# Attention and two gated layers in float32 parts: the products with w1, w2 and w_in by Strassen's scheme

## The chip, the cores and the metric

One core of a Trainium2 chip runs the whole program. The metric is device microseconds from start to end of one launch. The engines are named as in the profile: PE (TensorE matmuls) with PEld (its weight loads), DVE (VectorE), ACT (ScalarE), POOL (GpSimd) and SP (SyncE, which issues the transfers).

## The reference

```
scores = q @ k^T / 8, causal mask, softmax over keys, @ v   # 2 batches x 12 heads, 448 tokens, width 64
x = heads side by side                  # 896 tokens x 768
x = ((x @ w1) * (x @ w2)) @ w3 @ w_out  # w1, w2 768x1024, w3 1024x1024, w_out 1024x768
g = relu(x @ w_in) ** 2                 # w_in 768x2048
out = g @ w_out2                        # 2048x768
```

The weights arrive as 64-bit floats and are rebuilt as 32-bit ones on the chip. Each large product is done in a float32 variant of PE (F32R) on operands split into a high and a low part, as three matmuls: high by high, high by low, low by high.

## The kernel before

**Attention and W.** Thirteen slots (the loop `for p in range(SLOTS)`) each handle one pair of heads: `scores(p)`, `minima` (DVE: mask and row extreme), `exps` (ACT), `divide` (POOL, or DVE for the last pair's second head), and for the pair before, `p_transposes` (PE, copied out by ACT) and `attend`, whose result `x_parts` (L285) splits into the two parts of `xT`, in slots of 448 tokens per batch. Between them PE computes W = w3 @ w_out in 32 half units (`w_half`, L293, of which `fill` hands out one or none at each of three places of a slot); DVE adds them into `wraw` in SBUF. The 16 pieces of w3 and 8 of w_out, and then the first of w1 and w2, are loaded and converted step by step (`step`, `convert`, L83): ACT and DVE rebuild float32 from the 64-bit words (L102, L103, L108), ACT casts the high part (L90), DVE subtracts for the low part (L106). In this stage PE, DVE and ACT each run in the order of the code (`manual_schedule`); POOL and SP, and everything later, are ordered by a planner.

**w1 and w2** (`w12`, `ab`). For each of 8 column blocks m, PE multiplies the 6 row blocks of w1, then those of w2, by both batches of `xT`, 3 matmuls of 448 columns each: 576 matmuls. ACT copies the w1 result out of PSUM (L489), DVE multiplies (L490), ACT casts (L119) and POOL subtracts (L120) into `abT`. The first two m take batch 0 first (`EARLY`), so that the last pair of heads is not yet needed.

**h** (`h_parts`). 288 matmuls of 448 columns, W against `abT`.

**Last layer.** Two groups of d_ff: 8 blocks of w_in (288 matmuls of 448 columns; ACT takes ReLU, square and high part, POOL the low part), then 336 matmuls of 384 columns with w_out2, added into `acc`.

Weights wait in a ring of 8 tiles of both parts; `used` converts the next one when one is free. Two groups begin with a `pause` (one float32 matmul of 64 columns).

Of the kernel before, what the change touches and what calls it, by code (L numbers as in the profile page):

```python
# [8 lines left out]
F32 = mybir.dt.float32  # L9
F32R = mybir.dt.float32r  # L10
# [7 lines left out]
def attention_moe_moe2(ctx: ExitStack, tc: tile.TileContext, qk, v, w1, w2, w3, w_out, w_in2, w_out2, out):  # L18

# [21 lines left out]
    KD = DM // P  # L41
    KF = w1.shape[0]
# [6 lines left out]
    RING = 8  # L49
# [11 lines left out]
    ringp = ctx.enter_context(tc.tile_pool(name="ring", bufs=RING))  # L61
    ps_w = ctx.enter_context(tc.tile_pool(name="ps_w", bufs=2, space=PSUM))
    rawp = ctx.enter_context(tc.tile_pool(name="raw", bufs=RAW))

    xT = big.tile([P, 2, KD, NT], F32R, tag="X", name="xT")
    wraw = big.tile([P, KF, DM], F32, tag="W", name="wraw")

    def mm(o, l, r, start, stop):
        return nc.tensor.matmul(o, l, r, start=start, stop=stop)  # L69


    raws, f32s = {}, {}
# [8 lines left out]
    def convert(a=None, b=None):  # L81

        if b:  # L83
            nm, n = b
            if nm == "w3":
                t = w3_tile(n)
            else:
                t = ringp.tile([P, 2, DM], F32R, tag="ring", name=f"hl_{nm}_{n}")
            x = wraw[:, n, :] if nm == "W" else f32s[b] if whole(b) else f32s.pop(b)
            nc.scalar.copy(t[:, 0], x)  # L90
            hls[b] = t
        if a:
            raw = raws.pop(a)
            n = raw.shape[1]
            low, high = raw[:, :, 0], raw[:, :, 1]
            if whole(a) and a[0] == "w3":
                y = w3_tile(a[1])[:, 0].bitcast(F32)
            elif whole(a):
                y = w3p[0].tile([P, DM], F32, tag="xw", name=f"xw_{a[1]}", bufs=NB)
            else:  # L100
                y = rawp.tile([P, DM], F32, tag="x", name=f"x_{a[0]}_{a[1]}", bufs=XB)[:, :n]
            nc.scalar.activation(y, high.bitcast(F32), AF.Prelu, scale=2.0 ** -112, alpha=-2.0 ** 32)  # L102
            nc.vector.tensor_scalar(low, low, 2.0 ** -29, 7.0, ALU.mult, ALU.min)  # L103
            f32s[a] = y
        if b:
            nc.vector.tensor_tensor(t[:, 1], x, t[:, 0].bitcast(F32), op=ALU.subtract)  # L106
# [4 lines left out]
    def whole(key):  # L111

        return key[0] == "w3" and key[1] < PLAIN or key[0] == "wout" and key[1] < NB

    def w3_tile(n):
        return w3p[0].tile([P, 2, W3N], F32R, tag="w3", name=f"w3_{n}", bufs=2)
# [23 lines left out]
    order += ring[KF:]  # L140
    source = {"wout": w_out, "w1": w1, "w2": w2, "w3": w3, "win2": w_in2, "wout2": w_out2}
    place = {key: i for i, key in enumerate(order)}
    in_ring = {key: i for i, key in enumerate(ring)}
    hls = {}
    made = {"load": 0, "f32": 0, "hl": 0}

    def make_loads(n):
        for key in order[made["load"]:n]:
            if key[0] != "W":
                load(key, source[key[0]][key[1]])  # L150
        made["load"] = max(made["load"], min(n, len(order)))

    def make_f32(n):
        for key in order[made["f32"]:n]:
            make_loads(made["f32"] + 1)
            if key[0] != "W":
                convert(key)
            made["f32"] += 1

    def make(key):  # L160

        while made["hl"] <= place[key]:
            i = made["hl"]
            at = order[i]
            make_f32(i + 2)
            make_loads(i + 2 + RAW)
            convert(b=at)
            made["hl"] += 1

    def used(key):  # L170

        n = in_ring[key] + RING
        if n < len(ring):
            make(ring[n])

    w3p = []


    with (
        tc.tile_pool(name="attq", bufs=2) as attq,  # L180
        tc.tile_pool(name="att", bufs=2) as att,
        tc.tile_pool(name="attc", bufs=1) as attc,
        tc.tile_pool(name="ps_a", bufs=6, space=PSUM) as ps_a,
    ):
        ident = attc.tile([P, P], F32, tag="ident", name="ident")
# [112 lines left out]
        w3p.append(attc)  # L298
        x_t = {}

        def w_half(g, i, n):
# [3 lines left out]
            for f in range(NB):  # L305
                c = slice(f * P, (f + 1) * P)
                if n3 < PLAIN:
                    mm(acc, f32s["w3", n3][:, c], f32s["wout", f][:, cols], f == 0, f == NB - 1)
                    continue
                t, wo = hls["w3", n3], hls["wout", g * NB + f]  # L310
                for s, r in ((0, 0), (0, 1), (1, 0)):
                    mm(acc, t[:, s, c], wo[:, r, cols],
                       f == 0 and (s, r) == (0, 0), f == NB - 1 and (s, r) == (1, 0))
# [6 lines left out]
        units = [(g, i, n) for g in range(N3 // KF) for i in range(KF) for n in range(2)]  # L320
        NU = len(units)


        parts = [key for key in order if not (key[0] == "w3" and key[1] < PLAIN)]
        steps = [0, 0]

        def free(key):
# [3 lines left out]
            k = in_ring.get(key, 0) - RING  # L331
            return k < 0 or k < NB and done[1] >= NU // 2

        def ahead(n):

            last = max(order.index(key) for key in LENT)
            return max(n + RAW, min(n + RAW + len(LENT), last + 1 + RAW))

        def step(f32=True, split=True):
            a, b = order[steps[0]], parts[steps[1]]  # L340
            spare = sum(not whole(k) for k in f32s) < XB
            b = b if split and b in f32s and free(b) else None
# [270 lines left out]
```

## Time and profile before

| | |
|---|---|
| three runs | 577.06, 577.17, 577.54 us; median 577.17 |
| profiled execution | span 575.4 us from first to last instruction; its own time is not listed apart, the median run stands 1.8 us above this span |
| granted PE clock | 1.000 on the mean |
| attention and W | 0 to 163.2 us |
| w1, w2 | 163.2 to 280.2 us |
| h | 280.2 to 338.5 us |
| last layer | 338.5 to 572.1 us, then the last add and the last store |

The page gives busy time by engine, the span in 40 slices, the chain of work that ended last, and the costliest groups. A group has line, engine, operation, result and inputs, shapes and count; behind the bar stand total busy time, mean ns of one, and the idle time before. Neighbouring instructions of an engine overlap at their ends, so the step from one start to the next is a little shorter than a duration.

### The profile page before, as it was taken

To read this page: it belongs to the slowest core of one execution; us is meant where nothing else is said; L and a number is where in the kernel's file an instruction comes from. 1 tells how busy PE (TensorE), PEld (TensorE's weight loads), DVE (VectorE), ACT (ScalarE), POOL (GpSimd) and SP (SyncE) were. 2 spreads that over 40 slices of the span, in tenths; PEclk is the share of its full clock that TensorE was granted. 3 is DMA by queue.
4 is the path that set the end of the run, shared out by engine and by line. 5 is a ranking of instruction groups with operands and counts; after the bars stand their busy time and mean duration, and the time that the engine had idled before them with its cause. 6 is when DMAs were issued, how large, how long until landed. Compare 5 with 4: busy or idle time off the path is not lost.

```text
span 575.4 us, 8129 instructions
## 1 busy us (share of the span) xinstructions
PE 563.9 (98%) x3144; PEld 506.5 (88%) x3144; DVE 281.3 (49%) x567; ACT 268.2 (47%) x574; POOL 159.1 (28%) x140
## 2 busy tenths in 40 slices
PE   7899999999999999999999999999999999999997
PEld 5557777778989999999999999999999999999997
DVE  5987887767687544222210484555102854421011
ACT  5778777757865533222210456666002666640000
POOL 3367677776200312111100003333000023330000
PEclk9999999999999999999999999999999999999999
DMA  8854554233266633000000274333100763000111
GB/s 318 288 194 140 177 159 159 84 124 120 88 225 245 204 120 107 9 1 1 1 1 0 67 271 156 109 111 110 56 1 4 270 219 110 1 1 29 56 55 56
DMA packets 14823, 63.96 MB, mean 111 GB/s; under 512 B 1665, under 2 KB 1921, under 8 KB 14785
## 3 DMA queue, kind: packets, MB, share of 16 engines
q1 hardware_dynamic: 14784, 63.45, 32.2%
q8 instruction: 25, 0.41, 0.3%
q14 instruction: 14, 0.11, 0.1%
HBM read 60.69 MB, written 2.75 MB: 110 GB/s over the span
## 4 chain that ended last, share of the span: by engine, by line
PE 86%; DVE 6%; ACT 5%; issue 1%; DMA 1%; DVEq 0%; ACTq 0%
PE w L69 28%; PE g L69 20%; PE o L69 20%; PE h L69 10%; PE s L69 3%; PE x L69 2%; PE pp L273 2%; ACT p L245 2%; ACT pt L277 2%; DVE p L238 1%; DVE xw L108 1%; DMA qk<-in_qk 1%; ACT hl_wout L90 1%; DVE raw_wout L103 0%; DVE x_wout L108 0%
## 5 line engine op out<-in xcount | busy, mean ns | idle before, releaser
L69 PE MATMUL g<-hT,hl_win 128*128 128x448 f32 x576 | 117.2, 365 | 0.0
L69 PE MATMUL w<-xT,hl_w 128*128 128x448 f32 x576 | 117.0, 365 | 0.0
L69 PE MATMUL o<-hl_wout,gT 128*128 128x384 f32 x672 | 116.9, 334 | 0.0
L69 PEld LDWEIGHTS o<-hl_wout,gT 128*128 128x128 f32 x672 | 116.6, 188 | 0.1
L69 PEld LDWEIGHTS g<-hT,hl_win 128*128 128x128 f32 x576 | 108.1, 188 | 8.5
L69 PEld LDWEIGHTS w<-xT,hl_w 128*128 128x128 f32 x576 | 108.1, 188 | 8.5
L255 POOL TENSOR_SCALAR p<-p,st 112x448 f32<-112x448 f32 (+1 forms) x84 | 96.5, 1166 | 51.9 <-DVE st L252 23.3
L120 POOL TENSOR_TENSOR gT<-r,gT 128x448 fp32r<-128x448 f32 x32 | 39.1, 1245 | 195.8 <-ACT gT L119 128.7
L69 PE MATMUL w<-hl_wout,w 128*128 128x384 f32 x336 | 64.4, 342 | 0.5 <-DVE w L106 0.3
L245 ACT ACTIVATE p<-p,st 112x448 f32<-112x448 f32 (+1 forms) x96 | 49.7, 530 | 27.1 <-DVE st L238 27.0
L69 PEld LDWEIGHTS w<-hl_wout,w 128*128 128x128 f32 x336 | 57.4, 188 | 3.9 <-issue 0.9
L69 PE MATMUL h<-abT,hl_W 128*128 128x448 f32 x288 | 58.5, 365 | 0.0
L69 PEld LDWEIGHTS h<-abT,hl_W 128*128 128x128 f32 x288 | 54.1, 188 | 4.3
L120 POOL TENSOR_TENSOR abT<-a,abT 128x448 fp32r<-128x448 f32 x16 | 21.8, 1377 | 111.8 <-ACT abT L119 111.8
L238 DVE CUSTOM_DVE_ANT_0 p<-s,mask 112x448 f32<-112x448 f32 (+1 forms) x96 | 36.5, 441 | 7.0 <-PE s L69 7.0
L106 DVE TENSOR_TENSOR hl_wout<-x_wout,hl_wout 128x768 fp32r<-128x768 f32 x20 | 19.1, 957 | 37.9 <-ACT hl_wout L90 37.9
L533 ACT ACTIVATE r<-g 128x448 f32<-128x448 f32 x32 | 15.8, 542 | 40.8 <-PE g L69 40.8
L69 PE MATMUL s<-qk 64*112 64x448 f32 (+3 forms) x192 | 28.6, 443 | 4.1 <-DMA qk<-in_qk 4.1
L560 DVE TENSOR_TENSOR acc<-o,acc 128x384 f32<-128x384 f32 x14 | 7.2, 553 | 49.0 <-PE o L69 49.0
L273 PE MATMUL pp<-ident,p 112*112 112x112 f32 x240 | 27.9, 262 | 3.3 <-DVE st L238 1.6
L102 ACT ACTIVATE x_w<-raw_w 128x768 f32<-128x768 f32 (+1 forms) x30 | 24.4, 815 | 13.7 <-DVE hl_w L106 10.9
L273 PEld LDWEIGHTS pp<-ident,p 112*112 112x112 f32 x240 | 23.5, 134 | 8.0 <-issue 2.8
(62 smaller groups left out, 538.0 us busy)
## 6 DMA issues: line engine op xcount, KB each, us to landing
raw_wout<-in_w_out SPq DMA_DIRECT2D x24, 768.0 KB, 4.5
raw_w<-in_w SPq DMA_DIRECT2D x16, 768.0 KB, 4.3
raw_win<-in_w_in SPq DMA_DIRECT2D x16, 768.0 KB, 4.2
raw_w<-in_w SPq DMA_DIRECT2D x16, 512.0 KB, 3.9
qk<-in_qk SPq DMA_DIRECT2D x12, 448.0 KB, 5.1
v<-in_v SPq DMA_DIRECT2D x12, 224.0 KB, 2.6
out<-acc SPq DMA_DIRECT2D x6, 384.0 KB, 2.3
out<-acc SPq DMA_DIRECT2D x2, 192.0 KB, 1.8
```

Source lines behind the costliest of these rows:

```text
L69: return nc.tensor.matmul(o, l, r, start=start, stop=stop)
L90: nc.scalar.copy(t[:, 0], x)
L102: nc.scalar.activation(y, high.bitcast(F32), AF.Prelu, scale=2.0 ** -112, alpha=-2.0 ** 32)
L106: nc.vector.tensor_tensor(t[:, 1], x, t[:, 0].bitcast(F32), op=ALU.subtract)
L120: (engine or nc.vector).tensor_tensor(lo, x, hi.bitcast(F32), op=ALU.subtract)
L238: nc.vector.tensor_tensor_reduce(e, ps[j, i], mask[:, S - (i + 1) * CP:], QS, 3.0e38, ALU.add, ALU.min, st_t[p][:, 0, j, i:i + 1],)
L245: nc.scalar.activation(e, e, AF.Exp, bias=st_t[p][:, 0, j, i:i + 1], scale=-1.0, accum_out=st_t[p][:, 1, j, i:i + 1])
L255: engine.tensor_scalar(e, e, st[:, 3, i:i + 1], None, ALU.mult)
L273: nc.tensor.transpose(x[:CP, o:o + CP], pt[:, off[i] + c * CP:off[i] + (c + 1) * CP], ident[:CP, :CP],)
L277: nc.scalar.copy(t[:, coff[g[0]]:coff[g[0]] + o], x[:CP, :o])
L533: nc.scalar.activation(r, o[b], AF.Relu)
L560: nc.vector.tensor_tensor(a, o[n], a, op=ALU.add)
```

## The change

One level of Strassen's scheme (Winograd's form) in the products with w1, w2 and w_in. Two column blocks m and m+1 form a pair; the weight is cut in 2x2 blocks (m or m+1 by rows 0 to 383 or 384 to 767) and the moving operand in 2x2 blocks (rows of x by batch). Seven block products of 9 matmuls of 448 columns take the place of 8 such. POOL forms the weight sums S1 to S4, DVE the operand sums T1 to T4, and DVE adds the products from three PSUM banks of a pair in SBUF.

`xT` becomes blocks B11, B12, B21, B22 (float32 sums kept during attention, high and low parts made from them after it). The ring has 8 slots of half width. `wraw` is written to DRAM piece by piece behind the second `w_half` of each piece and read back before h; the ring is filled by a plan of the uses (`pump`). The h stage goes by halves of rows and by batches. The last layer has four groups of 4 column blocks (63 x 2 products, then 168 matmuls of 384 columns). In `fill` the W units end one place earlier (`TAIL`). `EARLY` is gone. After attention only PE keeps the order of the code; DVE, ACT, POOL and SP are planned.

```diff
-    RING = 8
+    SLOTS8 = 8
+    TAIL = 1
-    EARLY = 2
+    fsp = ctx.enter_context(tc.tile_pool(name="fs", bufs=12))
+    w_dram = tc.dram_tile([KF, P, DM], F32, name="w_dram")
+    ring = big.tile([P, SLOTS8, 2, HN], F32R, tag="ring", name="ring")
+    xs = big.tile([P, 6, DM], F32, tag="xs", name="xs")
...
+    TWO = ("P1", "P6", "P5", "Q1", "P7", "P3", "Q6", "Q5", "P2", "P4", "Q7", "Q3", "Q2", "Q4")
+    A_OF = {"1": "A11", "2": "A12", "3": "S4", "4": "A22", "5": "S1", "6": "S2", "7": "S3"}
+    B_OF = {"1": "B11", "2": "B21", "3": "B22", "4": "T4", "5": "T1", "6": "T2", "7": "T3"}
+    CHAIN = {"1": "a", "2": "a", "6": "b", "7": "b", "4": "b", "5": "c", "3": "c"}
...
+    def sums(it):
+        which, nm, m = it
+        p, q = in_slot((nm, m)), in_slot((nm, m + 1))
+        t = in_slot(it)
+        a, b = t[:, :HN], t[:, HN:]
+        if which == "S12":
+            nc.gpsimd.tensor_tensor(b, q[:, :HN], q[:, HN:], op=ALU.add)
+            nc.gpsimd.tensor_tensor(a, b, p[:, :HN], op=ALU.subtract)
+        else:
+            nc.gpsimd.tensor_tensor(a, p[:, :HN], q[:, :HN], op=ALU.subtract)
+            nc.gpsimd.tensor_tensor(b, p[:, HN:], in_slot(("S12", nm, m))[:, :HN], op=ALU.subtract)
...
         def x_parts(p):
-            hi, lo = (xT[:, s, kk, b * S:(b + 1) * S] for s in range(2))
-            two_parts(hi, lo, x_t.pop(p))
+            if (b, h) == (0, 0):
+                xf["B12", k] = f_tile(f"xB12_{k}")
+                nc.scalar.copy(xf["B12", k], x)
+            elif (b, h) == (0, 1):
+                two_parts(xB["B22"][:, 0, k], xB["B22"][:, 1, k], x)
+                xf["T3", k] = f_tile(f"xT3_{k}")
+                nc.vector.tensor_tensor(xf["T3", k], x, xf["B12", k], op=ALU.subtract)
+            elif (b, h) == (1, 0):
+                two_parts(xB["B11"][:, 0, k], xB["B11"][:, 1, k], x)
+                xf["T2", k] = f_tile(f"xT2_{k}")
+                nc.vector.tensor_tensor(xf["T2", k], x, xf["T3", k], op=ALU.add)
+                t1 = xf["T1", k] = xf.pop(("B12", k))
+                nc.vector.tensor_tensor(t1, t1, x, op=ALU.subtract)
+            else:
+                xf["B21", k] = f_tile(f"xB21_{k}")
+                nc.scalar.copy(xf["B21", k], x)
...
                 nc.vector.tensor_tensor(dst, acc, dst, op=ALU.add)
+                if n == 1:
+                    nc.sync.dma_start(out=w_dram[i], in_=wraw[:, i])
...
+            if f32 and not a and (kept + made["item"] < XB or made["item"] >= XB):
+                more |= item_of()
+            if split and not b and post_ready():
+                more |= unit_of(-1)
+            convert(**more)
+            if split and not b and post_ready():
+                simple_items()
+                convert(**unit_of(-1))
...
-            n = max(0, done[0] - LEAD) * NU // (GAPS * SLOTS - LEAD) - done[1]
+            n = min(NU, max(0, done[0] - LEAD) * NU // (GAPS * SLOTS - LEAD - TAIL)) - done[1]
...
+        def product(self, n, pair, first_of_all):
+            o, t, b = st[chain], hls[A_OF[n], pair], self.B[B_OF[n]]
+            for k in range(KH):
+                for s, r in ((0, 0), (0, 1), (1, 0)):
+                    mm(o, t[s][:, k * P:(k + 1) * P], b[:, r, k],
...
+            if n == "1":
+                st["s1"] = t_tile(f"{name}s1")
+                nc.scalar.copy(st["s1"], o)
+            elif n == "6":
+                st["s2"] = t_tile(f"{name}s2")
+                add(st["s2"], o, st["s1"], op=ALU.add)
+            elif n == "5":
+                st["s3"] = t_tile(f"{name}s3")
+                add(st["s3"], o, st["s1"], op=ALU.add)
+            elif n == "7":
+                add(st["s3"], o, st["s3"], op=ALU.add)
+                self.out_of(nm, m + 1, 0, st["s3"], False)
+            elif n == "3":
+                add(st["s2"], o, st["s2"], op=ALU.add)
+                self.out_of(nm, m, 0, st["s2"], False)
+            elif n == "2":
+                self.out_of(nm, m, 1, o, True)
+            else:
+                add(st["s1"], o, st["s1"], op=ALU.add)
+                self.out_of(nm, m + 1, 1, st["s1"], False)
...
+    more_blocks("x", xB)
+    for n in ("T2", "T1", "T3"):
+        for k in range(KH):
+            x = xf[n, k] if n == "T2" else xf.pop((n, k))
+            block_parts(xB, n, k, x, nc.gpsimd if n == "T3" else None)
+    for k in range(KH):
+        x = xf.pop(("B21", k))
+        block_parts(xB, "B21", k, x)
+        t2 = xf.pop(("T2", k))
+        nc.vector.tensor_tensor(t2, x, t2, op=ALU.subtract)
+        block_parts(xB, "T4", k, t2)
...
+        (nc.vector if in_psum else nc.gpsimd).tensor_tensor(a, x, a, op=ALU.mult)
+        two_parts(*(ab[m][:, s, b * S:(b + 1) * S] for s in range(2)), a, nc.gpsimd)
...
+    w12 = Pairs(xB, ab_out)
+    with tc.manual_schedule(engines={ET.PE}):
+        pump(-1)
+        for at, (kind, what, which, used) in enumerate(plan):
+            if kind == "product":
...
+            pump(at)
```

## Rows read from the trace of the kernel before

**Rows 1.** The page, busy time: share of the span and instructions.
```profile
PE 563.9 (98%) x3144; PEld 506.5 (88%) x3144; DVE 281.3 (49%) x567; ACT 268.2 (47%) x574; POOL 159.1 (28%) x140
```

**Rows 2.** The chain that ended last: start us, us, what.
```profile
21.65 0.54 DVE xT L120
...
80.99 0.62 DVE xT L120
...
156.79 2.11 PE w L69 x12
158.90 2.04 PE x L69 x16
160.94 119.26 PE w L69 x590
280.20 58.36 PE h L69 x288
338.57 58.37 PE g L69 x288
...
455.20 58.60 PE g L69 x290
513.80 58.28 PE o L69 x336
```

**Rows 3.** Stretches: us, busy time (instructions) by engine, clock, DMA share, GB/s.
```profile
163.40:177.60 14.20, 14.20 (x72) 13.16 (x71) 12.85 (x17) 9.52 (x12) 1.16 (x1) 1.00 0.74 246
0.00:88.00 88.00, 79.83 (x502) 57.50 (x502) 69.21 (x212) 65.55 (x178) 53.10 (x51) 1.00 0.63 209
88.00:163.20 75.20, 75.17 (x528) 61.82 (x529) 54.66 (x165) 53.87 (x153) 45.03 (x43) 1.00 0.37 124
163.20:280.20 117.00, 117.00 (x580) 108.44 (x579) 51.82 (x68) 42.72 (x64) 19.17 (x14) 1.00 0.30 103
```

**Rows 4.** Groups by shape: busy us, mean ns of one, idle before.
```profile
L106 DVE TENSOR_TENSOR hl_W<-wraw,hl_W 128x768 fp32r<-128x768 f32 x8 | 7.6, 952 | 21.0 <-ACT hl_W L90 21.0
L90 ACT CAST hl_w<-x_w 128x768 fp32r<-128x768 f32 x16 | 13.4, 840 | 6.2 <-PE w L69 4.7 <-DVE x_w L108 1.5
L490 DVE TENSOR_TENSOR a<-w,a 128x448 f32<-128x448 f32 x16 | 9.4, 619 | 19.9 <-PE w L69 19.9
L119 ACT CAST xT<-x 128x448 fp32r<-128x448 f32 x12 | 6.3, 527 | 7.2 <-PE x L69 7.2
```

**Rows 5.** By line: duration ns min/median/max, first and last start us.
```profile
L108 DVE SCALAR_TENSOR_TENSOR x_win<-x_win,raw_win x16: 950/958/1914, 219.3 to 458.7; 128x768 uint32<-128x768 uint32 x16
L103 DVE TENSOR_SCALAR raw_win<-raw_win x16: 556/562/1269, 202.8 to 455.2; 128x768 uint32<-128x768 uint32 x16
L120 POOL TENSOR_TENSOR gT<-r,gT x32: 1151/1161/1482, 349.7 to 518.0; 128x448 fp32r<-128x448 f32 x32
```

**Rows 6.** Timeline of ACT and DVE near the end of attention.
```profile
150.49 1.19 DVE L255 TENSOR_SCALAR p<-p,st 112x448 f32<-112x448 f32 x4
151.59 0.55 DVE L316 TENSOR_TENSOR wraw<-w,wraw 128x384 f32<-128x384 f32 x1
153.78 0.95 ACT L102 ACTIVATE x_w<-raw_w 128x768 f32<-128x768 f32 x1
155.30 2.33 ACT L277 COPY pt<-pp 112x448 f32<-112x448 f32 x6 [0.56 <-PE pp L273]
```

**Rows 7.** Timeline of POOL and DVE, 363 to 367 us.
```profile
363.58 2.58 POOL L120 TENSOR_TENSOR gT<-r,gT 128x448 fp32r<-128x448 f32 x2 [5.01 <-issue]
364.08 1.08 DVE L103 TENSOR_SCALAR raw_wout<-raw_wout 128x768 uint32<-128x768 uint32 x1 [1.03 <-DMA raw_wout<-in_w_out]
365.08 1.91 DVE L108 SCALAR_TENSOR_TENSOR x_wout<-x_wout,raw_wout 128x768 uint32<-128x768 uint32 x1
```

**Rows 8.** DMA issues: KB each, median us from issue to landing.
```profile
raw_w<-in_w SPq DMA_DIRECT2D x16, 768.0 KB, 4.3
out<-acc SPq DMA_DIRECT2D x6, 384.0 KB, 2.3
```

More of the change, by code (lines that the diff above doesn't have):

```diff
@@ L109, in convert @@
                 y.bitcast(U32), y.bitcast(U32), 3, low, op0=ALU.logical_shift_left, op1=ALU.bitwise_or)
[L111 to L116, printed above, removed]
-    def two_parts(hi, lo, x, engine=None):
-        nc.scalar.copy(hi, x)
-        (engine or nc.vector).tensor_tensor(lo, x, hi.bitcast(F32), op=ALU.subtract)
-    ring = [("wout", f) for f in range(KF)]
@@ new lines, in try_load, with next_item @@
+    def try_load():
+        i = made["load"]
+        if i < len(loads) and sum(k in raws for k in loads[max(0, i - 2):i]) < 2:
+            load(loads[i], rawp, "raw")
+            made["load"] += 1
+            return True
+        return False
+    def next_item(floor=-1):
+        i = made["item"]
+        if i == len(items):
+            return None
+        it = items[i]
+        if x_before[it] >= made["unit"] or (it[0] in source and it not in raws):
+            return None
+        return it
@@ new lines, in simple_items, with item_of @@
+    def simple_items():
+        while (it := next_item()) and it[0] not in source:
+            if it[0] == "W":
+                _, i, half = it
+                nc.sync.dma_start(
+                    out=halves(in_slot(it)),
+                    in_=w_dram[2 * i:2 * i + 2, :, half * HN:(half + 1) * HN].rearrange("i p c -> p i c"))
+            else:
+                sums(it)
+            items_made.add(it)
+            made["item"] += 1
+    def item_of():
+        simple_items()
+        it = next_item()
+        if it is None:
+            return {}
+        made["item"] += 1
+        items_made.add(it)
+        return {"a": it, "y": in_slot(it)}
@@ L139, in attention_moe_moe2, with whole @@
                 order += [("wout", i + 1)]
[L140 to L176, printed above, removed]
+    def whole(key):
+        return key[0] == "w3" and key[1] < PLAIN or key[0] == "wout" and key[1] < NB
+    parts = [key for key in order if not (key[0] == "w3" and key[1] < PLAIN)]
     with (
+        tc.tile_pool(name="rawb", bufs=1) as rawb,
         tc.tile_pool(name="attq", bufs=2) as attq,
+        tc.tile_pool(name="attw", bufs=1) as attw,
+        tc.tile_pool(name="ringb", bufs=4) as ringb,
+        tc.tile_pool(name="attc", bufs=1) as attc,
         tc.tile_pool(name="att", bufs=2) as att,
-        tc.tile_pool(name="attc", bufs=1) as attc,
         tc.tile_pool(name="ps_a", bufs=6, space=PSUM) as ps_a,
     ):
+        wraw = attw.tile([P, KF, DM], F32, tag="W", name="wraw")
         ident = attc.tile([P, P], F32, tag="ident", name="ident")
@@ L316, in w_half @@
                 nc.vector.tensor_tensor(dst, acc, dst, op=ALU.add)
+                if n == 1:
+                    nc.sync.dma_start(out=w_dram[i], in_=wraw[:, i])
             else:
                 nc.vector.tensor_copy(dst, acc)
[L320 to L325, printed above, removed]
+        w_units = [(g, i, n) for g in range(N3 // KF) for i in range(KF) for n in range(2)]
+        NU = len(w_units)
+        steps = [0, 0, 0, 0]
         def free(key):
@@ L435, in attention_moe_moe2 @@
                 fill()
-        assert not units and all(k in hls for k in ring[:KF])
-        made.update(f32=steps[0], hl=steps[1] + PLAIN)
-        for f in range(KF):
-            used(("wout", f))
-    tmp = ctx.enter_context(tc.tile_pool(name="tmp", bufs=4, reuse_waits="tile"))
+        assert not w_units and steps[0] == len(order) and steps[1] == len(parts)
+    xt = ctx.enter_context(tc.tile_pool(name="xt", bufs=1, reuse_waits="tile"))
     big2 = ctx.enter_context(tc.tile_pool(name="big2", bufs=1, reuse_waits="tile"))
+    tmp = ctx.enter_context(tc.tile_pool(name="tmp", bufs=1, reuse_waits="tile"))
```

475 lines of the change are left out of this document (328 added, 147 removed).

## The prediction

> **What bounds the kernel now.** First the busy times: PE 98% of the span, the next engine 49% [rows 1]. A busy PE need not be a full one, so next the chain of waits: from 160.9 us to the end it is PE alone, in steps that are exact multiples of a matmul [rows 2]: h takes 58.36 us for 288 matmuls of 448 columns, 0.2026 us each; the w_out2 part 58.28 for 336 of 384 columns, 0.1735 each. Then the stretches: PE has no gap from 88 us on (75.17 of 75.20 us busy), while before 88 us it is idle 8 us and DVE leads, 69.2 of 88 us [rows 3]. So after 163 us a matmul removed is time removed as long as ACT, DVE and POOL keep up; they have room there, DVE 51.8 and POOL 19.2 of the 117 us with w1 and w2 [rows 3]. The question is how much of that room the change takes, and when.
>
> **What it removes.** A pair of column blocks needs 7 x 9 = 63 matmuls of 448 columns for 72. There are 4 pairs of w1, 4 of w2, 8 of w_in: 16 x 9 = 144 matmuls, 144 x 0.2026 = 29.2 us. The nine of a product go one after another into one bank; the trace has that pattern in the first two m, one batch alone: 72 matmuls in 14.20 us, 0.197 each by a count good to one matmul or two [rows 3]. So the pitch stays. h and the w_out2 part keep their counts of 288 and 672. Two `pause`s more (four for two) cost what the second w_in group has over the first, 58.60 - 58.37 = 0.23 us each [rows 2]: +0.5. Net on PE: -28.7 us, all on the path.
>
> **Attention up to slot 11.** `x_parts` loses a DVE subtraction of 0.54 us for pairs 0 to 2 and 9 to 11, and gains one for 3 to 5 and two for 6 to 8. Four such subtractions stand on the chain, pairs 0, 1, 3 and 4 (first and last of the four in [rows 2]): two go, two of about 0.55 come. The later ones fall where PE is full and DVE has 20 of 75 us free [rows 3]. I take 0, bounds -1.5 and +1.5. The eight stores of `wraw` and their reading back (384 KB each, 2.3 us [rows 8]) lie beside PE; SP's queue holds the stores between loads made many slots ahead: 0, up to +1.
>
> **The hand-over to the first products.** This is where I expect the loss. `fill` now ends one place earlier, so from slot 7 on every piece of attention comes one half unit of W, 2.1 us, later against the same PE work, and PE would reach the first product at 163.0 as before. But the last steps of attention now hold things in the fixed order of ACT and DVE that wait for POOL. On the time axis of before, with the durations of [rows 4 to 6] and, estimated from them by width, 0.48 us for a 384-column DVE low part (952/2), 0.42 for its ACT cast, 1.0 for a POOL sum of 384 columns (1161 x 384/448):
> - DVE's last `divide` moves from 150.5 to 153.1 (2.1, and 0.5 for a w3 cast now ahead of the exponentials); behind it the W add 0.55, the rebuild of w1's block 1 (0.56 and 0.96) and a low part: 156.6. POOL then makes S1 and S2: 158.6. ACT's cast of S2 waits for them, and behind it in ACT stands the copy of pair 10 out of PSUM: 159.5. The last half unit wants that bank at 158.9: 0.6 us.
> - ACT goes on with the S1 cast, the rebuild of w2's block 0 (0.95, then DVE 0.96), its cast, and only then the six copies of the last transposes (2.33): the fourth at 163.8. The last `attend` could start at 161.6: 2.0 us or a little more.
> - The W add of the last half unit stands in DVE behind a second rebuild: 164.5 + 0.42 + 0.95 + 0.96 + 0.48 + 0.55 = 167.9. The first product takes that bank; PE is ready at 165.8: 2.1 us.
> - T2's parts lie where `wraw` was, so they wait for its last store: 167.9 + 2.3 = 170.2, or up to 2 us later behind a 768 KB load (4.3 us) issued just before [rows 8]. One cast (0.53) and three low parts follow; product 1 ended at 170.0. Second product: 1.2 to 3.2 us late.
> Sum 5.9 to 7.9; bounds 1 (the planner and POOL better than I think) and 9; I take 6.5. In before nothing of this existed: the first two m were taken by batch 0, and there is no gap at 163 [rows 2].
>
> **The first pairs.** The fifth product (P7) goes into the bank of the second, which DVE must have added out. Ahead of that add in the code stand 15 block operations (0.56 each, by width), two rebuilds and some low parts, 11.5 us from 170.2; PE gets there near 176.7. If the planner keeps code order: +5.6; if it takes what is ready: 0. I take 2.5.
>
> **DVE and POOL together.** The timeline shows that they exclude each other on operands in SBUF: while POOL's two subtractions run to 366.16, a DVE rebuild begun at 365.08 takes 1.91 us and ends 0.83 after POOL, where its median is 0.96 [rows 5, 7]; the operation before it took 1.08 for 0.56. In the 102 us of w1 and w2 POOL now has 26 sums (1.0 each), 12 products and 19 low parts (1.16): 62 us, where 19 stood. DVE has there, with two SBUF operands or of the kind that was held up, 48 + 4 low parts (23 + 4 us), 14 rebuilds (1.4 each with their overlap, 20) and the 15 block operations (8): 55 us, besides 40 adds and 4 multiplications out of PSUM that don't collide. 62 + 55 = 117 against 102. About 8 of POOL's can run on into h. From T2's arrival at 170.2, 109 us end at 279; PE's 55 products of 1.82 end at 271. So 0 (what is late is not needed yet: the ring runs 8 products, 14.6 us, ahead) to 8; I take 4.
> The Trainium skill, page "SBUF — State Buffer", section "Who interferes with whom", says that GpSimd and a VectorE instruction with two SBUF inputs hold one port pair in turn, each for its whole instruction. By that rule alone the stage would be 117 us of that port; the trace agrees on the single case (1.91 us).
>
> **h and the last layer.** h gains 8 sums and 12 low parts on POOL, 22 us of 58: hidden. A group of the last layer has, in its 25.6 us of products, about 13 us of POOL and 17 of such DVE work, but half of that serves w_out2 and may slip into the next 29 us: 0, up to 1 each, 4 in all. Last add and store are as before.
>
> **Sum.** 575.4 - 28.7 + 6.5 + 2.5 + 4 = 559.7 us of span. The median run stands 1.8 above the profiled span: 561.5 us.
>
> **Rivals.**
> 1. The hand-over is smooth. For it: the planner ordered DVE, ACT and POOL well around 163 us before, and only about 2 us of stall would remain if POOL's sums come early. Against: ACT and DVE are in fixed order there. 577.2 - 28.7 + 2 = 550.5.
> 2. DVE and POOL bind the stage with w1 and w2 throughout. For it: 117 us of exclusive work; adds that free banks queue behind operations held by POOL, with 3.7 us (two products) to spare. Against: no such wait of PE in the trace, where DVE was busy 12.9 of 14.2 us [rows 3]. h would begin at 170.2 + 117 = 287 instead of 265.6 after the gains: +21.6 in place of 13, and 1 in some groups: 571.
> 3. Slower: each of the 16 pairs holds PE for its sums, because ACT and DVE stop in order at the cast of S2, with the adds behind it. Price 2.0 for the sums and 0.4 for the cast, 2.4 x 16 = 38: 577.2 - 28.7 + 38 = 587. It decides from 28.7/16 = 1.8 us a pair. Against: after attention the order is planned, and sums are made a pair ahead.
> 4. PE is not the limit that it seems (a slower pitch of the new products, or a lower clock behind the gaps) and the gain is eaten: near 577.
>
> **How the numbers follow.** Forecast 0.50, rival 1 0.22, rival 2 0.20, rival 3 0.05, rival 4 0.03. The forecast's own range is 555 to 567. Half of rival 1 lies above 550, most of rival 2 below 573: range 550 to 573. A run tells 0.2% (1.2 us) from no change. Faster 0.92; same 0.02; slower 0.06.
>
> **What would show it.** PE's matmuls of 448 columns fall to 504 with w1 and w2 and 504 with w_in at 0.2026 us; the h chain stays 58.4 us. Waits of PE appear only near the hand-over: `attend` for ACT's copies, the first product for a DVE add, the second for T2, the fifth for a DVE add; 6 to 12 us together. POOL operations of 384 columns take 1.0 us alone and DVE low parts stretch beside them. Wrong would be: more than 5 us of PE waits after 190 us, a last layer that is not shorter by 14 us than 233.5, or a hand-over without gaps.

## The result and the profile after

The changed kernel takes 585.22 us (584.09 to 588.20) where the kernel before takes 577.36: ratio 1.0143, 95% interval 1.0118 to 1.0168. It is slower, and 23.7 us above the forecast. The profiled execution took 585.41 us, 583.6 of them from first to last instruction.

First the page, busy time and granted clock, beside [rows 1]:

```profile
PE 546.6 (94%) x3004; PEld 485.7 (83%) x3004; DVE 406.8 (70%) x770; ACT 312.4 (54%) x685; POOL 282.0 (48%) x231
...
PEclk9999999999987999898999999999999998999999
```

PE has lost 17 us of busy time but its share fell from 98 to 94%: work was taken off it and gaps came in. DVE went from 281 to 407 us, POOL from 159 to 282. And the clock row has eights and a seven where it was 1.000 throughout.

Then the stretches, cut where PE starts each stage (columns as in [rows 3]): the first pair of blocks of w1 and w2 (14 products), the second, third and fourth, h, the last layer.

```profile
166.90:204.09 37.19, 29.85 (x129) 26.14 (x129) 32.50 (x50) 19.34 (x38) 21.08 (x15) 0.86 0.35 117
204.09:236.03 31.94, 27.54 (x127) 24.58 (x126) 28.83 (x37) 13.50 (x26) 20.88 (x17) 0.95 0.31 99
236.03:266.44 30.41, 27.62 (x128) 24.65 (x127) 25.59 (x33) 13.07 (x25) 19.20 (x16) 0.95 0.31 104
266.44:292.34 25.90, 25.90 (x128) 23.98 (x126) 16.20 (x22) 10.85 (x20) 12.39 (x10) 0.98 0.41 122
292.34:350.70 58.36, 58.36 (x289) 54.09 (x288) 27.37 (x38) 22.00 (x38) 28.06 (x23) 1.00 0.17 55
350.70:580.30 229.60, 222.38 (x1183) 212.54 (x1181) 149.93 (x211) 114.08 (x208) 79.20 (x59) 0.99 0.30 101
```

At 0.2026 us a matmul, the 126 of a stretch with 14 products need 25.5 us; the first adds a pause of 0.23. So the four lose 11.4, 6.4, 4.9 and 0.4 us. h is what it was [rows 2]. The last layer needs 504 x 0.2026 + 672 x 0.1735 + 0.7 = 219.4 and loses 10.2. With the 3.9 us by which the first product starts later than 163.0, where the prediction has PE arrive if it never waits, 37.2 us are lost; the prediction had priced 13 (6.5, 2.5 and 4). DVE is busy 28.8 of 31.9 us in the second stretch.

What PE waited for, longest first (total, times, longest):

```profile
PE w_0b L65 <- ACT xT L68: 5.6, 1, 5.6
...
PE o L65 <- POOL gT L69: 2.6, 2, 2.3
PE win_10b L65 <- DVE win_10s L701: 2.6, 1, 2.6
PE w_2b L65 <- DVE w_2s L696: 2.4, 1, 2.4
...
PE x L65 <- ACT pt L412: 1.6, 1, 1.6
...
PE w_0c L65 <- DVE w_0s L699: 1.2, 1, 1.2
PE w L65 <- ACT xB L447: 0.9, 1, 0.9
PE w_0a L65 <- ACT xB L447: 0.6, 1, 0.6
```

Beside the hand-over (5.6, 1.6, 0.9, 0.6) stands a kind that the forecast had in the first pairs only: products of the bank "b" (L65) that wait for a DVE addition, L696 behind P6 or L701 behind Q7. (P and Q are the two pairs of a stretch, the digit is the block product, in the order of `TWO` in the diff.) Both additions read a bank into which PE writes again after two other products. Left out are five more of that kind (2.2, 2.0, 1.5, 0.6 and 0.5 us).

How one such wait comes about, on the timeline of PE, DVE, POOL and ACT:

```profile
205.91 1.99 PE L65 MATMUL w_2b<-xT,ring 128*128 128x448 f32 x9
...
209.06 0.91 ACT L92 ACTIVATE xs<-raw_w 128x768 f32<-128x768 f32 x1 [1.26 <-POOL xs L244]
...
209.96 1.16 POOL L69 TENSOR_TENSOR abT<-a,abT 128x448 fp32r<-128x448 f32 x1
210.00 1.93 DVE L98 SCALAR_TENSOR_TENSOR xs<-xs,raw_w 128x768 uint32<-128x768 uint32 x1 [1.02 <-ACT xs L92]
211.07 1.84 POOL L741 TENSOR_TENSOR w_0s<-w_0s,w_0s 128x448 f32<-128x448 f32 x1
211.85 1.48 DVE L96 TENSOR_TENSOR ring<-xs,ring 128x384 fp32r<-128x384 f32 x1
213.25 0.61 DVE L696 TENSOR_TENSOR w_2s<-w_2b,w_2s 128x448 f32<-128x448 f32 x1
213.92 2.09 PE L65 MATMUL w_2b<-xT,ring 128*128 128x448 f32 x9 [2.38 <-DVE w_2s L696]
```

P6 is in its bank at 207.7. The addition takes 0.61 us but starts 5.5 us later: ahead of it in DVE's order stands a rebuild (L98) that waits for ACT, and ACT for a sum on POOL; then the rebuild takes 1.93 us and a low part 1.48, with POOL at work beside both. PE gives the addition two products, 3.6 us.

Some of the gaps cost twice. Behind the first, a stretch and the starts of the products show the half clock:

```profile
174.80:182.30 7.50, 6.91 (x19) 5.77 (x19) 7.50 (x14) 7.50 (x16) 4.70 (x2) 0.53 0.32 106
```

```profile
176.11 3.35 PE L65 MATMUL w_0b<-xT,ring 128*128 128x448 f32 x8 [0.59 <-DVE xT L69]
179.26 3.20 PE L65 MATMUL w_0c<-xT,ring 128*128 128x448 f32 x9
182.30 1.99 PE L65 MATMUL w_0a<-xB,ring 128*128 128x448 f32 x9
184.12 1.98 PE L65 MATMUL w_0b<-xT,ring 128*128 128x448 f32 x9
...
232.80 3.44 PE L65 MATMUL w_2b<-xT,ring 128*128 128x448 f32 x9 [2.02 <-DVE w_2s L701]
236.03 2.20 PE L65 MATMUL w_4a<-xB,ring 128*128 128x448 f32 x9
```

From 179.26 to 182.30 is 3.04 us for nine matmuls, and 1.82 for the next nine. At a granted clock of 0.53, close to 1.2 of 2.4 GHz, products take 1.7 to 1.9 times as long. Five did (8 of 9 matmuls at 176.11, and those at 179.26, 232.80, 263.35 and 492.74: 3.15, 3.04, 3.23, 3.09 and 3.35 us from start to start, 15.9 for 8.9 at full clock): 7.0 us. Two other gaps of that size, 2.38 us before 213.92 and 2.35 us before 384.41, were followed by a granted clock of 1.00.

### The profile page after: what moved, and what is told of

Read it like the earlier page. It is cut to its first block, busy times and chain, and to the rows that moved or that the text cites. A ratio compares the mean times of both kernels' runs of the same rounds, so it can differ in the third digit from the quotient of the medians.

```text
span 583.6 us, 8340 instructions
## 1 busy us (share of the span) xinstructions
PE 546.6 (94%) x3004; PEld 485.7 (83%) x3004; DVE 406.8 (70%) x770; ACT 312.4 (54%) x685; POOL 282.0 (48%) x231
## 4 chain that ended last, share of the span: by engine, by line
PE 59%; DVE 15%; ACT 10%; DMA 6%; POOL 5%; issue 4%; DVEq 0%; ACTq 0%; POOLq 0%
PE o L65 18%; PE h L65 10%; PE w L65 8%; DVE ring L96 4%; DVE xs L98 3%; PE s L65 3%; DMA raw_wout<-in_w_out 3%; ACT xs L92 3%; PE x L65 2%; PE pp L408 2%; ACT p L380 2%; ACT pt L412 2%; PE w_6b L65 2%; PE w_4b L65 2%; DMA raw_w<-in_w 2%
## 5 line engine op out<-in xcount | busy, mean ns | idle before, releaser
L96 DVE TENSOR_TENSOR ring<-xs,ring 128x384 fp32r<-128x384 f32 (+1 forms) x140 | 118.4, 858 | 34.4 <-ACT ring L87 34.2
L87 ACT CAST ring<-xs 128x384 fp32r<-128x384 f32 (+1 forms) x140 | 78.4, 577 | 96.9 <-PE o L65 44.9
L65 PE MATMUL o<-ring,gT 128*128 128x384 f32 x672 | 117.9, 335 | 2.6 <-POOL gT L69 2.6
L65 PEld LDWEIGHTS o<-ring,gT 128*128 128x128 f32 x672 | 116.5, 188 | 3.6 <-POOL gT L69 3.3
L65 PE MATMUL h<-abT,ring 128*128 128x448 f32 x288 | 58.5, 365 | 0.0
L65 PEld LDWEIGHTS h<-abT,ring 128*128 128x128 f32 x288 | 54.1, 188 | 4.3
L65 PE MATMUL w<-hl_wout,w 128*128 128x384 f32 x192 | 36.2, 340 | 0.9 <-ACT xB L447 0.9
L65 PEld LDWEIGHTS w<-hl_wout,w 128*128 128x128 f32 x192 | 32.9, 188 | 2.4 <-ACT xB L447 1.1
L65 PE MATMUL s<-qk 64*112 64x112 f32 (+3 forms) x192 | 28.5, 432 | 4.5 <-DMA qk<-in_qk 4.4
L98 DVE SCALAR_TENSOR_TENSOR xs<-xs,raw_w 128x768 uint32<-128x768 uint32 (+1 forms) x30 | 27.1, 904 | 5.8 <-ACT xs L92 5.7
L412 ACT COPY pt<-pp 112x336 f32<-112x336 f32 (+1 forms) x72 | 27.7, 477 | 1.8 <-PE pp L408 1.8
L65 PEld LDWEIGHTS s<-qk 64*112 64x112 f32 x192 | 15.9, 185 | 15.1 <-issue 6.0
L65 PE MATMUL w<-ring,w 128*128 128x384 f32 x144 | 27.9, 343 | 0.3 <-DVE w L96 0.3
```

Source lines behind the costliest of these rows:

```text
L65: return nc.tensor.matmul(o, l, r, start=start, stop=stop, **more)
L87: nc.scalar.copy(t[0], x)
L96: nc.vector.tensor_tensor(t[1], x, t[0].bitcast(F32), op=ALU.subtract)
L98: nc.vector.scalar_tensor_tensor(y.bitcast(U32), y.bitcast(U32), 3, low, op0=ALU.logical_shift_left, op1=ALU.bitwise_or)
L412: nc.scalar.copy(t[:, coff[g[0]]:coff[g[0]] + o], x[:CP, :o])
```

## The experiments

Theory A: the sums on POOL cost the time. They keep DVE company, DVE slows, its additions come late, PE waits and then runs at half clock. Rivals: the order of the products (two products between Q7 and Q4), the hand-over, or a PE slower for another reason.

**Sums on DVE, the order of products, no sums, and the two engines alone.**

```diff
# sums on DVE
-            nc.gpsimd.tensor_tensor(b, q[:, :HN], q[:, HN:], op=ALU.add)
+            nc.vector.tensor_tensor(b, q[:, :HN], q[:, HN:], op=ALU.add)
# order: Q6 ahead of P7, Q7 ahead of P4
-    TWO = ("P1", "P6", "P5", "Q1", "P7", "P3", "Q6", "Q5", "P2", "P4", "Q7", "Q3", "Q2", "Q4")
+    TWO = ("P1", "P6", "P5", "Q1", "Q6", "P7", "P3", "Q5", "P2", "Q7", "P4", "Q3", "Q2", "Q4")
# no sums: S1 to S4 are plain blocks (the sums are left out)
-            "S2": (("S12", nm, m), lo), "S1": (("S12", nm, m), hi),
+            "S2": ((nm, m), lo), "S1": ((nm, m + 1), lo),
-            "S3": (("S34", nm, m), lo), "S4": (("S34", nm, m), hi),
+            "S3": ((nm, m), hi), "S4": ((nm, m + 1), hi),
```

> The four weight sums of each pair are made by DVE instead of POOL; all else as in the changed kernel (585.2 us). Theory A (DVE and POOL shut each other out on operands in SBUF, and their common time bounds the stage with w1 and w2): 26 sums of about 1.2 us on POOL become 26 of about 0.5 us on DVE there, 18 us less of common time, so the stage falls from 125 us to 110 to 118 and the whole to 572 to 578. Theory B (it is DVE's queue alone that is too long, or the distance of two products between the reads and the next use of a PSUM bank): DVE gets 64 x 0.5 = 31 us more work, the waits of PE grow, 585 to 592. Theory C (the loss is the serial hand-over from attention): only the link through POOL shortens, 582 to 584.

580.23 us, ratio to before 1.0054 (1.0029 to 1.0078): 5 us better than the changed kernel. It lies in no theory's range; it is the direction of A and half its size, and against B, whose 585 to 592 it misses although DVE has more to do. The sums (64 in all, 4 for each of 16 pairs, not 62 as the later expectation has it) take 0.64 to 0.75 us there, some 44 us more for DVE, which is then busy 57.4 of the 62 us from 204 to 266. A sum costs on either engine.

> The fourteen products of two pairs in another order (P1 P6 P5 Q1 Q6 P7 P3 Q5 P2 Q7 P4 Q3 Q2 Q4), so that at least three products instead of two lie between the last use of a PSUM bank and the next; work unchanged. Theory B: the waits of the second product chain for DVE adds (2.4, 2.0, 0.6, 2.2 us with w1 and w2, 0.5, 1.5, 2.6 in the last layer) and the half clock behind some of them go, 570 to 576. Theory A: DVE and POOL have the same work and PE waits elsewhere for the same time with w1 and w2; only the last layer, which has slack, gains some 5 us: 578 to 582. Theory C: no change beyond 2 us.

588.90 us, 1.0195 (1.0172 to 1.0219). The stage with w1 and w2 does shorten, 116.3 us from its first product to h instead of 125.4, but the first product starts 3.8 us later (4.6 us of waiting for a copy by ACT), and in the last layer the w_out2 part waits 10.0 us for `gT`, 5.7 for ACT and 4.3 for POOL. It lies above every theory's range. The distance between the products does matter to the stage, but the 9.1 us that the stage gains are lost before and behind it: the waits move, and the order alone does not bring the time back.

> The weight sums are left out: the units S1 to S4 are taken from the plain weight blocks, so 64 POOL operations go and DVE, ACT and PE keep theirs. Theory A: 26 x 1.2 = 31 us of common time leave the stage with w1 and w2; it falls from 125 to 106 to 112 us, DVE's 384-column low parts fall from 0.75 us towards 0.55, the whole 564 to 572. Theory B (DVE's own queue and the bank distance): DVE's work is the same, 580 to 586. Theory C (hand-over): ACT's wait of 5.7 us for POOL goes and nothing later changes, 579 to 583.

562.66 us, 0.9751 (0.9732 to 0.9769), a little below A's 564 to 572 and far from B and C. Taking the sums away takes 22.6 us away. Without them PE waits in the second to fourth stretch for less than half a us each time. The same 62 us (204 to 266; the kernel without sums is 7 to 17 us further on there), first the changed kernel, then the one without sums:

```profile
204.00:266.00 62.00, 54.81 (x253) 48.94 (x252) 54.13 (x70) 26.66 (x52) 39.73 (x32) 0.95 0.31 102
```

```profile
204.00:266.00 62.00, 61.60 (x301) 56.00 (x300) 46.21 (x73) 27.57 (x54) 20.06 (x15) 1.00 0.36 115
```

301 matmuls for 253, with 73 DVE operations for 70 in 46.2 us instead of 54.1. DVE's groups in this stretch, in the same order:

```profile
L96 DVE TENSOR_TENSOR ring<-xs,ring 128x384 fp32r<-128x384 f32 x30 | 26.5, 884 | 1.8 <-ACT ring L87 1.8
L98 DVE SCALAR_TENSOR_TENSOR xs<-xs,raw_w 128x768 uint32<-128x768 uint32 x8 | 9.6, 1199 | 2.0 <-ACT xs L92 2.0
```

```profile
L96 DVE TENSOR_TENSOR ring<-xs,ring 128x384 fp32r<-128x384 f32 x33 | 23.9, 730 | 2.7 <-ACT ring L87 2.5
L98 DVE SCALAR_TENSOR_TENSOR xs<-xs,raw_w 128x768 uint32<-128x768 uint32 x6 | 5.7, 956 | 0.9 <-ACT xs L92 0.9
```

The additions out of PSUM take 0.61 to 0.62 us in both; what POOL's company stretches are the low parts and the rebuilds (their first step, L93, as well: 1069 ns against 563). A low part was priced at 0.48 and takes 0.88 in the mean (the shortest of the whole run took 0.54). Without the sums it falls to 0.73, not to the 0.55 that A had: other POOL work, 20.06 us of it, is still beside it. Even without sums DVE is busy 46 of 62 us, where the kernel before had 20.0 in the same window: half-width blocks make 56 low parts where 16 of double width stood, and each product brings an addition.

> Only this, nothing of the reference: on tiles of 128x384 in SBUF, 16 two-operand adds on DVE alone, 16 with one operand in PSUM, 16 with a scalar, 16 two-operand adds on POOL alone, and then POOL's 16 beside each of the DVE kinds. Theory A: alone DVE 0.5 us, POOL 1.0 us; beside POOL the DVE add from SBUF and the scalar form stretch to about 1.4 us each (they take turns), the one from PSUM does not stretch. If they only share bandwidth or not at all: DVE 0.5 to 0.8 us beside POOL in all three kinds.

The timeline of this kernel (start, us for all, count at the end; everything of the computation is left out but the listed operations):

```profile
4.33 9.45 DVE L33 TENSOR_TENSOR v<-x 128x384 f32<-128x384 f32 x16
13.69 9.43 DVE L37 TENSOR_TENSOR vp<-acc,x 128x384 f32<-128x384 f32 x16
23.04 6.27 DVE L41 TENSOR_SCALAR vc<-x 128x384 f32<-128x384 f32 x16
...
30.46 15.97 POOL L45 TENSOR_TENSOR g<-x 128x384 f32<-128x384 f32 x15
...
48.13 19.56 DVE L33 TENSOR_TENSOR v<-x 128x384 f32<-128x384 f32 x16 [1.10 <-POOL g L45]
48.17 19.10 POOL L45 TENSOR_TENSOR g<-x 128x384 f32<-128x384 f32 x15
...
68.27 18.89 DVE L37 TENSOR_TENSOR vp<-acc,x 128x384 f32<-128x384 f32 x32
...
87.55 23.40 DVE L41 TENSOR_SCALAR vc<-x 128x384 f32<-128x384 f32 x32
```

Alone, a DVE addition of 384 columns takes 0.59 us and one on POOL 1.06. Together with both operands in SBUF, DVE takes 1.22 and POOL 1.27. With one operand in PSUM (`acc`) DVE keeps its 0.59 beside POOL. That is A's picture, with less stretching than its 1.4. So a low part that meets a POOL operation takes twice its time, and an addition out of PSUM doesn't; the additions are late because they stand behind the others.

**Sums made, but read by nobody.** This is to take apart two ways in which a sum can cost: by being made, and by being read.

```diff
-            "S2": (("S12", nm, m), lo), "S1": (("S12", nm, m), hi),
+            "S2": ((nm, m), lo), "S1": ((nm, m + 1), lo),
-            "S3": (("S34", nm, m), lo), "S4": (("S34", nm, m), hi),
+            "S3": ((nm, m), hi), "S4": ((nm, m + 1), hi),
+        if it[0] in ("S12", "S34"):
+            return max(n_unit[u] for u in units if not wide(u) and u[1] == it[1:])
```

> Left out: the S units read plain blocks of the weights; the 62 sums are still made on POOL, in the same slots, but nobody reads them. Theory A (it is the company that POOL's sums keep DVE that costs the time: DVE's instructions with two operands in SBUF wait out POOL's): near the changed kernel, 577 to 587 us, with low parts of 384 columns still at 700 ns or more in the mean. Rival (it is the way through the sums that costs: cast and low part of an S unit wait for two or three sums in a row on POOL): near the kernel without sums, 562 to 569.

581.29 us, 1.0064 (1.0047 to 1.0080): theory A's range, and the low parts of 384 columns took 927 ns in the mean in the same 62 us, as A had them (700 or more). On the whole, making the sums costs 18.6 us of the 22.6 (581.29 less 562.66). That is their company, POOL's queue, and also the slots of `xs` that they hold, which the run without sums leaves free; no run takes the slots apart from the rest. In the profiles ACT's rebuilds wait for a slot about as long either way (from 204 to 292 us: 14.4 us in the changed kernel, 11.2 without sums, 18.4 with sums unread). By stage the picture is less simple (starts of PE in the timelines, in us; the last column needs no trace: matmuls at full pitch from 163.0):

| | changed | sums unread | no sums | sums on DVE | full pitch |
|---|---|---|---|---|---|
| first product starts | 166.9 | 166.0 | 163.3 | 165.6 | 163.0 |
| first stretch | 37.2 | 38.6 | 33.7 | 36.7 | 25.8 |
| second to fourth | 88.3 | 81.3 | 77.9 | 84.3 | 76.6 |
| h | 58.4 | 58.4 | 58.4 | 58.4 | 58.4 |
| last layer | 229.6 | 231.6 | 223.6 | 232.7 | 219.4 |

In the second to fourth stretch making the sums costs 3.4 us (81.3 less 77.9), and reading them 7.0 more. Of these 7.0, PE's waits are 3.5 (7.2 us in the changed kernel, 3.7 with sums unread), and 2.7 are the half clock behind two gaps; with sums unread the longest gap there, 2.04 us, was not followed by it. Why reading costs 3.5 us of waits is not shown: in these stretches ACT waits for POOL's sums only twice, 2.4 us together, each time with a rebuild, as at 209.06 above. Before and around the first products, and in the last layer, making the sums costs all there is to see. In the last layer that has a second form, POOL's own queue. Two of PE's waits with sums unread, the first in the last layer, the second in the hand-over:

```profile
PE o L65 <- POOL gT L69: 6.9, 3, 3.4
PE w_0b L65 <- ACT xT L68: 4.6, 1, 4.6
```

and on the timeline of the changed kernel, POOL before the first w_out2 product that waits:

```profile
373.55 1.71 POOL L240 TENSOR_TENSOR xs<-xs 128x384 f32<-128x384 f32 x1
375.23 1.38 POOL L243 TENSOR_TENSOR xs<-xs 128x384 f32<-128x384 f32 x1
376.57 1.74 POOL L241 TENSOR_TENSOR xs<-xs 128x384 f32<-128x384 f32 x1
...
379.38 1.34 POOL L244 TENSOR_TENSOR xs<-xs 128x384 f32<-128x384 f32 x1
380.69 3.67 POOL L69 TENSOR_TENSOR gT<-win_2s,gT 128x448 fp32r<-128x448 f32 x2
...
384.41 24.54 PE L65 MATMUL o<-ring,gT 128*128 128x384 f32 x140 [2.35 <-POOL gT L69]
```

Four sums of the next group, 6.2 us, stand among the low parts of g that the product at 384.41 needs.

**The hand-over.** T2's blocks first in the memory that `wraw` leaves.

```diff
-        for n in ("T1", "T2", "T3", "T4", "B21"):
+        for n in ("T2", "T1", "T3", "T4", "B21"):
```

> The changed kernel with the tiles of T1 and T2 laid out in the other order, so that T2 no longer lies over the W units of attention whose last store to DRAM ends at about 172 us. Theory C (hand-over: the second product waits 5.6 us for T2 because of that store, and the half clock behind the gap costs 2.7 us more): the gap falls to 0 to 2 us, the second and third product run at full clock, 577 to 580 us. Rival (ACT's order holds T2 back: a rebuild of w1 that waits for its load until 173.1 us stands before T2's casts): the gap stays 4 to 6 us, 583 to 586.

586.38 us, 1.016 (1.0127 to 1.0193), and PE's wait is 5.0 + 0.8 us instead of 5.6 + 0.6. T2's place alone does not hold it. What stands ahead of T2's cast in ACT's order is the same in both kernels; of the changed one, with the last store of `wraw`:

```profile
168.78 0.33 SPq L473 DMA_DIRECT2D w_dram<-wraw  x1
...
171.41 0.93 ACT L87 CAST ring<-xs 128x384 fp32r<-128x384 f32 x2 [1.36 <-POOL xs L241]
173.14 0.93 ACT L92 ACTIVATE xs<-raw_w 128x768 f32<-128x768 f32 x1 [0.81 <-DMA raw_w<-in_w]
174.16 1.50 ACT L68 CAST xT<-xT 128x448 fp32r<-128x448 f32 x3
```

A cast that waits for a sum, then a rebuild that waits for a load, then T2. Load and memory hold T2 to the same moment: the rebuild behind the load ends at 174.07, and the store, issued at 168.78, took 5.2 us to land, so till 174.0. Taking away one leaves the other; with T2's place changed the rebuild still ends at 173.5, and T2's cast starts there. Both stand behind DVE: the load was issued at 167.84, when the rebuild before it on DVE had ended (167.81), the store behind the last addition into `wraw` (168.20 to 168.75). Without sums the load is issued at 162.83 and the store at 163.77, five us earlier each, and T2's wait is 3.8 us; with sums that nobody reads it is 4.6 and 1.3 more for DVE's part. So the wait of the cast at 171.41 is not what holds T2. A kernel with T2 ahead of the rebuild in ACT's order and off that memory was not run.

**w1 and w2 by eight block products, w_in by seven.** The w1 and w2 part of the change taken back, and with it its sums and the T blocks of the hand-over; the diff is cut to its core (the first blocks of m go by the halves of x that are ready first), first as it is, then with P4 and Q7 exchanged, then with the sums of w_in on DVE. In these three kernels, and in the first two of the next group, one or two blocks of w1 or w2 enter as zeros; every instruction is there.

```diff
-        two_pairs([("w1", 2 * d), ("w2", 2 * d)])
+        for m in (2 * d, 2 * d + 1):
+            for nm in ("w1", "w2"):
+                for half in range(2):
+                    for b in range(2):
+                        plain(nm, m, b, half)     # A[m % 2][half] times B[half][b], 9 matmuls
```

> Products with w1 and w2 by eight block products again (576 matmuls, no sums, no T blocks, results straight from PSUM), all else as in the changed kernel, Strassen with w_in kept. Theory A (DVE, held to POOL's pace, bounds the stage with w1 and w2 in the changed kernel, so its 72 saved matmuls bought nothing): DVE and POOL have room, the stage takes 117 to 119 us against 125.4, the whole 573 to 578, although PE has 14.6 us more to do. Theory that PE is still the bound: 585 + 14.6 = 600.

> As the kernel with plain w1 and w2, and in the last layer the products P4 and Q7 change places, so that three products instead of two lie between the read of Q7's bank and Q4. If the waits of Q4 (0.5, 1.5, 2.6 us and a half clock behind the last) are a matter of that distance: 3 to 6 us below that kernel. If they are DVE's and POOL's lateness, the w_out2 part waits for gT instead: within 2 us of it.

> As the kernel with plain w1 and w2, and the sums of w_in made by DVE instead of POOL. Theory A: in the last layer POOL is left with 8 low parts a group, DVE's low parts run near 0.55 us, the waits there (10.7 us in the changed kernel) fall by 3 to 6 us: 570 to 574. If DVE's queue counts alone, 16 us more of work on DVE lengthen them: 576 to 582.

575.67 us, 0.9961 (0.9947 to 0.9975); 576.71, 0.9982 (0.9961 to 1.0004); 574.64, 0.9947 (0.9927 to 0.9967). The first is A's 573 to 578: 72 matmuls more than the changed kernel, and 9.6 us faster. So Strassen's scheme on w1 and w2 as written, with its hand-over, costs 9.6 us net, though it takes 14.6 us off PE. What is left of the change, w_in above all, gains 1.9 and not 14.6. The exchange gains nothing that shows (the second lies within 2 us of the first), and DVE in POOL's place 1 us at most, which the spread of the runs does not tell from none; 574.64 lies between the two ranges given.

**The last layer eased.** Then, with the sums on DVE, the low parts of the second pair of each group's g go to DVE too; with and without the exchange; and last without the zeros.

```diff
-        two_parts(*(g_t[m % 4][:, s, b * S:(b + 1) * S] for s in range(2)), r, nc.gpsimd)
+        two_parts(*(g_t[m % 4][:, s, b * S:(b + 1) * S] for s in range(2)), r, nc.gpsimd if m % 4 < 2 else None)
```

> w1 and w2 by eight block products, w_in by seven with its sums on DVE, and the low parts of the second pair of each group's g on DVE instead of POOL. Theory A (what is left in the last layer are o's waits for POOL's low parts, 4.6 us in the run with the sums on DVE): 571 to 574 us. Rival (DVE has no room for them beside the sums, and the adds that Q4 waits for come later): 574 to 579.

> The same, with Q7 a product earlier and P4 a product later, so that Q4 comes three products behind Q7 instead of two. Theory A: the wait of Q4 for Q7's add (1.1 us, twice, in the run with the sums on DVE) goes, and 1 to 2 us with it: 570 to 573. Rival (as in the order tried for all pairs: the wait moves to o, which then waits for P4's part of g): 573 to 577.

> The version that the runs point to, whole: w1 and w2 by eight block products, w_in by seven with its sums on DVE, the second pair's low parts of g on DVE. Against the run before it (569.02 us) one block of w2 is cast behind its decoding instead of ahead of it, so that the block no longer enters as zeros; no instruction is added. Theory A (nobody waits for that cast): 568 to 570 us. Rival (the cast is late, the second product of the stage waits for it on PE, and the half clock follows): 570 to 574.

569.02 us, 0.9854 (0.9841 to 0.9867), two us better than A said. These three kernels also take the first blocks of w1 and w2 in another order than the ones above; by the profiles that is worth 0.5 us before the first product, while the last layer shortens by 4.6 (231.3 to 226.8). With the exchange it is 573.08, 0.9922 (0.9903 to 0.9941), its rival's 573 to 577, with 5.2 us of `o` waiting for ACT's part of `gT`. The last, whole, takes 570.60, 0.9867 (0.9844 to 0.9889); by its median that is the rival's 570 to 574, but no product waits for the cast in its profile, and its runs (568.13 to 572.11) don't tell it from 569.02. That version beats both kernels: 1.3% faster than before, 14.6 us faster than the changed one. Its page and its waits:

```profile
PE 555.3 (97%) x3076; PEld 493.4 (87%) x3076; DVE 351.7 (62%) x748; ACT 302.1 (53%) x656; POOL 154.3 (27%) x136
```

```profile
PE o L65 <- DVE gT L69: 1.5, 3, 1.2
...
PE win_6b L65 <- DVE win_6s L713: 0.7, 1, 0.7
```

POOL is back at 154 us and no wait is above 1.2 us after attention. Its last layer takes 225.7 us against 233.5 before: 7.8 of the 14.6 us are gained.

## Why the prediction was wrong

- **What bounds the kernel, and what is removed from PE: right.** 504 and 504 matmuls, 1.82 us for nine at full clock; h 58.4. What the sum left out is that the clock can fall behind gaps: five products behind four gaps of 2 us and more ran at about half of it, 7.0 us. Rival 4 named it, at 0.03.
- **Attention up to slot 11, 0: right, within 0.7 us.** The first product is 3.9 us late, 3.2 of it in three waits of the hand-over.
- **The hand-over, +6.5: the places right, one size wrong.** 0.9 (0.6 priced), 1.6 (2.0), 0.65 (2.1, and it was a copy by ACT that the product waited for, not a DVE addition); the second product 6.2, where 1.2 to 3.2 was priced. Sum 9.3, just over the bound of 9, and the half clock behind it, 2.7 more, was not priced. The term that was mis-sized is the store of `wraw`: issued at 168.8, not 167.9, and 5.2 us to land, where 2.3 with up to 2 us more stood. A rebuild that waits for its load, which the sum did not have ahead of T2, holds it as long.
- **The first pairs, +2.5: too much for the wait, but for another product.** P7 did not wait; P3 did, 1.2 us, for the addition behind P5.
- **DVE and POOL together, +4: the step that failed.** The second to fourth stretch alone lose 11.7 us. The durations were off (a low part 0.88 for 0.48, a sum 1.14 to 1.27 for 1.0): most of it is stretching, 0.59 to 1.22 for two additions that meet, as the kernel with the two engines alone shows. The slack that they were held against was wrong, too. "What is late is not needed yet: the ring runs 8 products, 14.6 us, ahead" is true of the weights and not of the additions, which stand in the same order on DVE behind the weights' operations and have two products. An operation that holds up an addition reaches PE after 3.6 us, not after 14.6; the addition at 213.25 was 5.5 us late. And the sum treated POOL's operations as so much time on a shared port; that the sums are read costs another 7.0 us in these stretches, as far as the run with sums unread tells.
- **h, 0: right. The last layer, taken as 0 and at most 4: wrong**, 10.2, the largest part of the miss. The slack fails here again: half of the work "may slip into the next 29 us", but the additions behind Q7 and the low parts of g may not. 6.0 of the 10.2 go with the sums, in part through POOL's own queue, where sums of the next group stand ahead of g's low parts; 4.2 stay without them.
- **The rivals.** Rival 2 is what happened: DVE and POOL set the pace of the stage with w1 and w2, additions queue behind operations held by POOL. It was priced with h at 287; h began at 292.3, since the half clock and the longer hand-over come on top, and the last layer was let off. It was judged at 0.20 on the ground that before had no such wait while DVE was busy 12.9 of 14.2 us [rows 3]; but there POOL was busy 1.2 of these 14.2 us, and PE took its eight banks in turn, so that none had to come free within two products. Rival 3's 587 lies nearest to the 585.22, by luck: no product of the changed kernel waits for the cast of a sum.

Two of the prediction's own signs of being wrong came: 14.4 us of PE's waits behind 190 us, where it allowed 5, and a last layer shorter by 3.9 us instead of 14.

Without the sums the same program takes 562.66 us, 1.2 above the forecast. That closeness is luck in part. The 13 us priced hold 4 for DVE and POOL together, of which by its own sum nothing would be left without the sums (117 less 26, so 91 us against 102), and the trace without sums loses 13.9 all the same (557.0 less the 543.1 of full pitch): 7.9 in the first stretch, 4.2 in the last layer. What is shown is the price of the 64 sums, 22.6 us, where the forecast had a part of 13.

Left open: whether T2 ahead of that rebuild would start the second product earlier; why reading the sums costs what it does; why h took 59.5 us in the profiled executions of the last version and of the first with plain w1 and w2, with a clock shown as 1.00; why a gap of 2.38 us (213.92) was followed by nine matmuls in 2.02 us and one of 2.02 us (232.80) by nine in 3.23.

## What to carry to other kernels

When work moves from a full engine to a half empty one, the room is not the idle share but the slack of the shortest wait queued behind it: list what each in-order engine must deliver, by when, and hold the lateness of everything ahead of it against that. Price an operation on DVE with its neighbour on POOL at work, not by its duration alone. And a gap on PE can be paid for again at half clock behind it, so a saving in matmuls has to be larger than the gaps by a margin.

## What was not expected of the hardware

Two-operand DVE instructions and POOL's are not strictly in turn. The Trainium skill, page "SBUF — State Buffer", section "Who interferes with whom", calls the port pair that the two share "an exclusive lock"; of DVE's 2-port modes it says that whoever issues first gets the pair for the whole instruction and the other "fully blocks". Sixteen of each in turn would be 9.45 + 16 x 1.065 = 26.5 us; both ended within 19.56, so they overlap in part, and DVE bears most of it (0.59 to 1.22, POOL 1.06 to 1.27). The same section's rule that a DVE instruction with at most one SBUF input, outside the 2-port modes, stays clear holds for the PSUM form (0.59 beside POOL). The `tensor_scalar` form, one SBUF input, did not stay clear: 32 took 23.40 us; with 16 at 0.39 after POOL's end, the other 16 took 17.1, 1.07 each, one for each POOL operation. The section names that form among those that can enter the 2-port modes and contend.

The length of a gap does not tell whether half clock follows. In the changed kernel it came behind gaps of 5.6, 2.6, 2.2 and 2.0 us, for one to two products, and not behind those of 2.38 and 2.35. With the sums of w_in on DVE and plain w1 and w2 a gap of 1.53 us was followed by a granted clock of 0.51 over 3.35 us; with sums unread one of 2.04 us by 1.00.
